# One TensorE-bound attention-and-MLP kernel: the decay row copied by DMA, two tiles mixed transposed, wide unread matmuls, and a new order

## The chip, the cores and the metric

The kernel runs on one core of a Trainium2 chip. A core has a matrix engine (TensorE, PE in the profile, with its weight loads shown apart as PEld), VectorE (DVE), ScalarE (ACT), GpSimd (POOL) and a queue engine (SyncE, SP) that issues most DMAs. TensorE writes to eight banks of PSUM; VectorE and ScalarE read them. Sixteen DMA engines move data between HBM and SBUF.

The metric is the time of one execution in microseconds. The kernel before has a median of 141.36 us in three runs (140.43 to 142.12).

## The reference

Two phases follow each other. The first is a linear attention with a decay per head and channel; the second mixes its output over tokens and channels.

```python
# B, H, S, D = 4, 8, 768, 48
for t in range(S):
    cur = u * k[t] (x) v[t]                    # outer product, D x D per head
    y[t] = r[t] @ (state + cur)
    state = w * state + k[t] (x) v[t]
x = y with the heads side by side              # B, S, 384
theta = x @ w_theta
zr, zi = x * cos(theta), x * sin(theta)
y2 = w_tok_r @ zr + w_tok_i @ zi               # mixes the 768 tokens
un = x + y2
out = un + relu(un @ w_ch)
```

The inputs and the output are float32; r, k and v hold 4.7 MB each, and so does the output.

## The kernel before

The 768 tokens of each of the 4 batches are worked in three groups of 256 tokens, so there are 12 groups, 0 to 11. The scan over time is turned into matmuls. For a group, k and r are multiplied by powers of w (tiles Kw and Rw, L554 and L556, by VectorE or GpSimd), turned by TensorE with an identity ("flip", L493; eight matmuls of 128 columns), copied out of PSUM to KT and RT (L503 on ScalarE, L504 on VectorE), and multiplied with each other ("scores", L605); a mask is applied on the way out (mAT, L614). "outer" (L671) makes the state's update, "diag" (L638) the bonus of u, and "states", "outputs" and "bonus" (L747 to L812) the group's rows of x. x is turned (xT), multiplied with w_theta (L835), and ScalarE takes sine and cosine (L842, L846); VectorE makes z (L850).

When a batch's three z are there, its six tiles of 128 tokens are mixed: 12 matmuls per tile (L872), stationary a 128 x 128 block of the token weights, moving 384 columns of z. VectorE adds x (un, L890), un is turned (uT; by a DMA transpose for groups 0 to 10, by TensorE for group 11), multiplied with w_ch ("chan", L905, three matmuls), and the result is put through relu, added to un and stored.

**The start.** The powers of w need w's logarithm on all 128 partitions. VectorE zeroes a tile (L300), one DMA on SP's queue brings the 1.5 KB of w into its first row (L302), and TensorE multiplies it with a tile of ones ("spread", L311, float32), which puts the row on every partition of a PSUM bank. ScalarE takes the logarithm (L389) and then the powers (L399).

**Unread matmuls.** `unread(k, n, wide)` (L291) issues n matmuls of a tile of zeros into a bank that nothing reads. They keep TensorE at work while it has nothing else to do. At the start there are two blocks ("warm"): 6 and 8 matmuls of 512 columns. The table IDLE puts more behind given tasks: 89 matmuls of 128 columns in all.

**The order.** Nothing is scheduled at run time. A planner, which is not part of the kernel, has written out four tables: ORDER (746 tasks, in the sequence in which they are issued to their engines), WAYS (which of a task's possible engines does it), BANKS (which PSUM bank each product takes) and AFTER (further waits, so that issue order and buffers agree). `Plan.issue` walks through ORDER. Each engine runs its own tasks strictly in that sequence: a task that waits holds up all that stands behind it on its engine. SP runs the loads, the DMA transposes and the stores in the same way. The numbers in `P.add(pe(ns, ...))` are the planner's costs; they do not act on the chip.

The loads go into a ring of 16 buffers (tile ld). In the order before, SP issues k of group 0, the row of w, r of group 0, w and u again for small tables, then r and k of group 1, v of group 0, k and r of group 2 and v of group 1.

**The end.** For group 11 the tiles are not turned by DMA but by TensorE: un on VectorE, flip (three matmuls), copy, chan, and one instruction on VectorE that does relu and the last sum (L920), then the store. On VectorE the last tasks stand in this sequence: un of one tile, a last sum of group 11, the copy of the turned tile, and three more last sums.

Of the kernel before, what the change touches and what calls it, by code (L numbers as in the profile page):

```python
# [30 lines left out]
WARM, WARM_NS = (6, 8), (1280, 1700)  # L31
# [5 lines left out]
ORDER = [  # L37
# [39 lines left out]
]  # L77
# [23 lines left out]


IDLE = [
    (5, 1, 21), (6, 2, 6), (7, 4, 3), (73, 5, 12), (75, 6, 5), (116, 7, 5), (78, 4, 11),
    (88, 6, 4), (124, 1, 3), (96, 7, 9), (107, 6, 7), (51, 6, 3),
]

# [868 lines left out]
```

## Time and profile before

| | |
|---|---|
| median of three runs | 141.36 us (140.43 to 142.12) |
| the profiled execution | 140.2 us |
| its span, first to last instruction | 138.4 us |
| matmuls, and as many weight loads | 1948 |
| busy: TensorE, VectorE, ScalarE, GpSimd | 129.0, 106.6, 81.6, 70.1 us |
| unread matmuls among TensorE's | 103, of which 14 are 512 columns wide |
| moved by DMA | 25.47 MB, 184 GB/s in the mean |

The span lies 1.8 us under the time of the same execution. A profile's busy time of TensorE counts matmuls that overlap each other once, and the length of a single matmul is modelled (326 ns for one that follows the next at 162 ns), so the pace is read from the distance of starts or from a long chain of equal matmuls. "issue" in a view is time in which an engine waited for nothing that the profile shows.

### The profile page before, as it was taken

How to read it: one execution, taken by the hardware profiler on the slowest of the kernel's cores; microseconds unless marked ns; L12 is line 12 of the kernel's file. 1: busy time of each engine (PE TensorE's matmuls, PEld its weight loads, DVE VectorE, ACT ScalarE, POOL GpSimd, SP SyncE). 2: the span in 40 equal slices, each digit the busy share in tenths (PEclk: the TensorE clock that was granted, in tenths of full speed). 3: DMA queues.
4: the chain of work that ended last, by engine and by line, in shares of the span. 5: the costliest groups of instructions: out<-in, count | busy, mean ns of one | idle time of the engine just before them, and what ended most of it. 6: DMA issues, size and time to landing. Idle time of an engine off the chain costs nothing.

```text
span 138.4 us, 4633 instructions
## 1 busy us (share of the span) xinstructions
PE 129.0 (93%) x1948; PEld 87.6 (63%) x1948; DVE 106.6 (77%) x197; ACT 81.6 (59%) x158; POOL 70.1 (51%) x79
## 2 busy tenths in 40 slices
PE   5999996999999969999999999999999999999970
PEld 2848775866776746776666667665657666566630
DVE  6247996889999676989698989799499999353180
ACT  3088878799858459747992174964540738910300
POOL 6003986090075875816546878670519973630310
PEclk9999999999999999999999999999999999999996
DMA  3999599999999971599999999999999792415244
GB/s 97 248 260 259 91 185 205 250 255 243 242 277 210 269 156 20 78 150 192 233 270 237 178 179 147 245 209 188 238 191 265 131 137 85 152 47 147 57 171 171
DMA packets 67199, 25.47 MB, mean 184 GB/s; under 512 B 61801, under 2 KB 67178, under 8 KB 67178
## 3 DMA queue, kind: packets, MB, share of 16 engines
q1 hardware_dynamic: 64746, 22.23, 73.8%
q0 software_dynamic: 2432, 2.95, 13.0%
q8 instruction: 15, 0.25, 0.7%
q14 instruction: 6, 0.05, 0.1%
HBM read 20.06 MB, written 4.72 MB: 179 GB/s over the span
## 4 chain that ended last, share of the span: by engine, by line
PE 75%; DVE 9%; ACT 4%; DMA 3%; issue 3%; POOL 1%; SPq 1%; DVEq 0%; POOLq 0%
PE bank L872 29%; PE bank L493 10%; PE bank L835 8%; PE bank L905 7%; PE bank L291 4%; PE bank L605 4%; DMA ld<-in_r_dram 3%; PE bank L671 3%; PE bank L760 2%; DVE Rw L554 2%; PE bank L812 2%; PE bank L776 2%; PE bank L638 2%; DVE mAT L614 1%; POOL Rw L554 1%
## 5 line engine op out<-in xcount | busy, mean ns | idle before, releaser
L872 PE MATMUL bank<-z,WrT 128*128 128x384 bf16 x144 | 46.9, 326 | 0.1
L872 PE MATMUL bank<-z,WiT 128*128 128x384 bf16 x144 | 46.8, 326 | 0.0
L915 POOL TENSOR_TENSOR fin_all<-fin_all,uu_all 128x384 f32<-128x384 f32 x20 | 17.9, 914 | 24.2 <-ACT fin_all L912 11.4
L554 POOL TENSOR_TENSOR Rw<-ld,rpow 128x768 bf16<-128x768 f32 x6 | 10.9, 1816 | 18.3 <-DVE mask L354 10.1
L614 DVE TENSOR_TENSOR mAT<-bank,mask 128x512 bf16<-128x512 f32 x28 | 18.3, 682 | 2.1 <-PE bank L605 2.0
L890 DVE TENSOR_TENSOR uu_all<-bank,x 128x384 bf16<-128x384 f32 x24 | 13.1, 554 | 8.9 <-PE bank L872 7.1
L872 PEld LDWEIGHTS <-WrT 128*128 128x128 bf16 x144 | 14.0, 98 | 8.1 <-DVE z L850 0.3
L872 PEld LDWEIGHTS <-WiT 128*128 128x128 bf16 x144 | 14.1, 98 | 7.7
L912 ACT ACTIVATE fin_all<-bank 128x384 f32<-128x384 f32 x20 | 9.5, 495 | 12.3 <-issue 8.1
L835 PE MATMUL bank<-Wth,xT 128*128 128x384 bf16 x72 | 14.8, 326 | 1.2 <-issue 1.2
L842 ACT ACTIVATE trig<-bank,pi 128x384 f16<-128x384 f32 x24 | 13.8, 592 | 1.0 <-PE bank L835 0.7
L905 PE MATMUL bank<-Wch,uu_all 128*128 128x384 bf16 x72 | 14.3, 326 | 0.0
L846 ACT ACTIVATE trig<-bank 128x384 f16<-128x384 f32 x24 | 11.9, 499 | 3.9 <-PE bank L835 2.6
L291 PE MATMUL bank<-zero 128*128 128x128 bf16 (+1 forms) x103 | 12.3, 275 | 1.7 <-DVE zero L298 1.7
L850 DVE TENSOR_TENSOR z<-x,trig 128x1536 bf16<-128x1536 bf16 x12 | 11.5, 962 | 2.7 <-ACT trig L846 2.6
L503 ACT ACTIVATE RT<-bank 128x1024 bf16<-128x1024 bf16 x12 | 12.4, 1030 | 2.1 <-PE bank L493 2.0
L614 DVE TENSOR_TENSOR mAT<-bank,mask_c 128x512 bf16<-128x512 f32 x20 | 13.0, 682 | 0.3 <-PE bank L605 0.3
L291 PEld LDWEIGHTS <-zero 128*128 128x128 bf16 x103 | 8.0, 111 | 5.0 <-issue 1.9
L503 ACT ACTIVATE KT<-bank 128x1024 bf16<-128x1024 bf16 x9 | 9.2, 1021 | 2.8 <-PE bank L493 2.8
L647 POOL TENSOR_TENSOR yd<-dg,vb 128x768 bf16<-128x768 f32 x7 | 10.3, 1475 | 0.8 <-DVE Rw L554 0.6
L554 DVE TENSOR_TENSOR Rw<-ld,rpow 128x768 bf16<-128x768 f32 x6 | 7.6, 1261 | 2.2 <-DMA ld<-in_r_dram 2.2
L905 PEld LDWEIGHTS <-uu_all 128*128 128x128 bf16 x72 | 6.5, 97 | 4.1 <-DVE uu_all L504 0.3
(114 smaller groups left out, 226.4 us busy)
## 6 DMA issues: line engine op xcount, KB each, us to landing
ld<-in_r_dram SPq DMA_DIRECT2D x12, 384.0 KB, 5.0
out_dram<-fin_all SPq DMA_DIRECT2D x11, 384.0 KB, 3.1
ld<-in_k_dram SPq DMA_DIRECT2D x7, 384.0 KB, 6.0
ld<-in_v_dram SPq DMA_DIRECT2D x7, 384.0 KB, 8.2
ld<-in_k_dram SPq DMA_DIRECT2D x10, 192.0 KB, 4.1
ld<-in_v_dram SPq DMA_DIRECT2D x10, 192.0 KB, 5.1
fin_all<-in_moe_w_tok_i_dram POOLq DMA_DIRECT2D x1, 384.0 KB, 5.0
x<-in_moe_w_tok_i_dram POOLq DMA_DIRECT2D x1, 384.0 KB, 7.6
```

What stands on the lines that cost most here:

```text
L291: ins = [nc.tensor.matmul(bank_t[k][:, :wide * C].rearrange("p (a c) -> p a c", a=wide), zero, bc(zero, 1, wide), start=True, stop=True, s ...
L493: ins = [nc.tensor.matmul(bank16(tok)[:, i * C:(i + 1) * C], s, ident, is_transpose=True, start=(i == 0), stop=(i == n - 1)) for i, s in e ...
L503: P.add([act(n * C, lambda: nc.scalar.activation(dst, src(), Act.Copy)), dve(n * C, lambda: nc.vector.tensor_copy(dst, src()), 1.0 if pair ...
L554: return eng.tensor_mul(to.rearrange("p j h d -> p h j d")[:, :, :, :D], tokens(i), pw)
L614: mask01[:, j] if pairs else mask_c): nc.vector.tensor_mul(
L835: ins = [nc.tensor.matmul(bank(th)[:, :HD], xT[:, t, dk, :], Wth[:, dk, :], start=(dk == 0), stop=(dk == ND - 1)) for dk in range(ND)]
L842: P.add(act(HD, lambda th=th, t=t, trig=trig: nc.scalar.activation(trig[:, t, 0], bank(th)[:, :HD], Act.Sin, bias=pi2), 144), use=[th], rd ...
L846: P.add(act(HD, lambda th=th, t=t, trig=trig: nc.scalar.activation(trig[:, t, 1], bank(th)[:, :HD], Act.Sin)), use=[th], rd=["sin"], wr=[( ...
L872: ins.append(nc.tensor.matmul(bank(tm)[:, :HD], (WrT, WiT)[ri][:, so, to * C:(to + 1) * C], z[:, so, ri], start=(part == 0 and i == 0), st ...
L890: P.add(dve(HD, lambda tm=tm, t=t, to=to, un=un: nc.vector.tensor_add(un[:, t], bank(tm)[:, :HD], x[:, to])), use=[tm], rd=[("x", xi, pr, ...
L905: ins = [nc.tensor.matmul(bank(tf)[:, :HD], uT[:, t, dk, :], Wch[:, dk, :], start=(dk == 0), stop=(dk == ND - 1)) for dk in range(ND)]
L915: P.add(pool(900, lambda t=t, un=un, fin=fin: nc.gpsimd.tensor_add(fin[:, t], fin[:, t], un[:, t])), rd=[("un", j, t)], wr=[("fin", j, t)] ...
```

## The change

1. **w by one DMA.** The row of w is read 128 times, by one DMA on ScalarE's queue, straight into 128 partitions of SBUF. The zeroing, the tile of ones and the matmul "spread" are gone, and the logarithm reads SBUF in place of PSUM.
2. **The last two tiles in transposed form.** For the two tiles of group 11, each mixing matmul of 384 columns becomes three of 128: stationary a block of z, moving the 128 columns of token weights. The product is un already turned. VectorE adds the turned x (xT) to give uT, which chan reads at once; TensorE turns uT back to un beside it, ScalarE copies that out, and the last sum reads it.
3. **Wide unread matmuls.** The block at the start is one of 10 matmuls of 512 columns. IDLE has 27 of 512 columns and 26 of 128 in place of 89 of 128.
4. **A new order.** ORDER (742 tasks), WAYS, BANKS and AFTER are new throughout. SP issues r of group 0, then k of groups 0 and 1, w and u for the small tables, v of group 0, r of group 1, k and r of group 2, v of group 1. VectorE zeroes the tile that the unread matmuls read as its second instruction. Group 0's r is worked before its k. At the end VectorE's sequence is the sum with xT, then four last sums.

```diff
-WARM, WARM_NS = (6, 8), (1280, 1700)
+(WARM,), WARM_NS = (10,), 2080
...
 IDLE = [
-    (5, 1, 21), (6, 2, 6), (7, 4, 3), (73, 5, 12), (75, 6, 5), (116, 7, 5), (78, 4, 11),
-    (88, 6, 4), (124, 1, 3), (96, 7, 9), (107, 6, 7), (51, 6, 3),
+    (3, 1, 6, 4), (3, 1, 2, 1), (71, 2, 8, 4), (71, 2, 1, 1), (26, 4, 3, 4), (26, 4, 2, 1),
+    (84, 0, 1, 4), (84, 0, 3, 1), (77, 6, 2, 4), (77, 6, 2, 1), (93, 5, 1, 4), (93, 5, 3, 1),
+    (155, 3, 1, 4), (155, 3, 3, 1), (117, 7, 1, 4), (117, 7, 3, 1), (98, 5, 1, 4), (98, 5, 1, 1),
+    (54, 5, 1, 4), (54, 5, 2, 1), (42, 0, 2, 4), (42, 0, 1, 1), (176, 1, 3, 1),
 ]
...
-            for k, n in idle.get(seq, ()):
-                unread(k, n)
+            for a, k, n, wide in idle:
+                if a == seq:
+                    unread(k, n, wide)
...
-        P.add((DVE, 250, False, lambda: nc.vector.memset(w_row, 0.0)), wr=["w_row"],
-              prio=-2.9e4, name="w zero")
-        P.add(sp(lambda: nc.sync.dma_start(out=w_row[:1], in_=rows_of(w, 1)), 400), wr=["w_row"],
-              prio=-1e4, desc=(0, 1, 65), name="w_row", kind="small")
-        P.add((DVE, 160, False, lambda: nc.vector.memset(ones, 1.0)), wr=["ones"], prio=-2.8e4,
-              name="ones")
+        P.add((ACT, 420, False, lambda: nc.scalar.dma_start(out=w_row, in_=rows_of(w, C))),
+              wr=["w_row"], prio=-1.2e4, desc=(2, 8, 70), name="w_row", kind="small")
...
-        P.add(pe(640, lambda: nc.tensor.matmul(
-            bank("w")[:, :HD], ones, w_row.rearrange("p h d -> p (h d)"), start=True, stop=True)),
-            rd=["w_row", "ones"], wr=["spread"], acq=["w"],
-            prio=-1e4, mode=4, name="spread")
...
-        P.add(act(HD, lambda: nc.scalar.activation(
-            lw_f, bank("w")[:, :HD].rearrange("p (h d) -> p h d", h=H), Act.Ln)), use=["w"],
-            rd=["set"], wr=["lw_f"], prio=-200, name="ln")
+        P.add(act_sb(HD, lambda: nc.scalar.activation(lw_f, w_row, Act.Ln)),
+              rd=["set", "w_row"], wr=["lw_f"], prio=-200, name="ln")
...
+                        def mix_t(tm=tm, to=to, part=part):
+                            ins = []
+                            for i in range(4):
+                                so, ri = 2 * part + i // 2, i % 2
+                                for dk in range(ND):
+                                    ins.append(nc.tensor.matmul(
+                                        bank(tm)[:, dk * C:(dk + 1) * C],
+                                        z[:, so, ri, dk * C:(dk + 1) * C],
+                                        (WrT, WiT)[ri][:, so, to * C:(to + 1) * C],
+                                        start=(part == 0 and i == 0 and dk == 0),
+                                        stop=(part == NP - 1 and i == 3),
+                                        skip_group_check=True))
+                            return ins[0], ins[-1]
...
+                    P.add(dve(HD, lambda tm=tm, t=t, uT=uT, xT=xT: nc.vector.tensor_add(
+                        uT[:, t], bank(tm)[:, :HD].rearrange("p (d c) -> p d c", d=ND),
+                        xT[:, t])), use=[tm], rd=[("xT", g % 2)], wr=[("uT", j, t)],
+                        prio=pb + 2 * t, name="un")
+                    flip(un[:, t].rearrange("p (d c) -> p d c", d=ND),
+                         [uT[:, t, dk, :] for dk in range(ND)], ("TU", g, t), pb + 4,
+                         [("uT", j, t)], [("un", j, t)])
+                    continue
...
-                if single:
-                    flip(uT[:, t], [un[:, t, dk * C:(dk + 1) * C] for dk in range(ND)],
-                         ("TU", g, t), pb + 4, [("un", j, t)], [("uT", j, t)])
-
...
-    P.issue(tc, ORDER, WAYS, BANKS, AFTER, dict((a, [(k, n)]) for a, k, n in IDLE), unread)
+    P.issue(tc, ORDER, WAYS, BANKS, AFTER, IDLE, unread)
```

More of the change, by code (lines that the diff above doesn't have):

```diff
@@ L89 @@
-BANKS = ("012345670134520642157630276145326437640516470627105426157321657635642561720436520514325073"
-    "514156714307142530617426137042137251376062501205713265726314652734105632761450146410416237"
-    "56367450261342507510735240735421736502413")
-AFTER = [
[6 rows of a table removed]
[39 rows of a table added]
+]
+WAYS = ("000000000000000000000000000000000000000010010100001001000000000001000000110000000000001100"
+    "100000000000000000000000002000000000000020002000010000000000000000000100000010000000000010"
+    "000000000000001002000000000000000020000000000000000000010100200000000000000010000000101000"
+    "000000011010000000000000000000010000000000000000000000000000000000000000000000000000000000"
+    "001100000000000100101010010000000000000000000000000000000000010000010000000000000000000000"
+    "000000000000000000000000000000000000000000000000000000000000000000000000000000000010000200"
+    "000010000010010000000000000000000000001000000000000100000000000000000000010000000000001001"
+    "000000001000000000000000000000000000000000000000000000000000000000000000000000000000000000"
+    "0000000000000000000000")
@@ L100 @@
+BANKS = ("012345670126304536175235014573654260451730452610526702467032034205420167251075320653712053"
+    "751463201753460210217301273625643515203150476513427605267014265730562540273145417141246315"
+    "026123540712034172564073125604721306452")
+AFTER = [
[6 rows of a table added]
 ]
 IDLE = [
-    (5, 1, 21), (6, 2, 6), (7, 4, 3), (73, 5, 12), (75, 6, 5), (116, 7, 5), (78, 4, 11),
-    (88, 6, 4), (124, 1, 3), (96, 7, 9), (107, 6, 7), (51, 6, 3),
[4 rows of a table added]
 ]
@@ L220 @@
     zero = sb.tile([C, C], BF16, name="zero")
-    ones = sb.tile([C, C], F32, name="ones")
     col_i = sb.tile([C, C], mybir.dt.int32, name="col_i")
@@ L308, in setup @@
         if WARM:
-            P.add(pe(WARM_NS[0], lambda: unread(P.bank_of["warm0"], WARM[0], 4)), rd=["zero"],
+            P.add(pe(WARM_NS, lambda: unread(P.bank_of["warm0"], WARM, 4)), rd=["zero"],
                   acq=["warm0"], prio=-2.1e4, name="warm")
-        P.add(pe(640, lambda: nc.tensor.matmul(
-            bank("w")[:, :HD], ones, w_row.rearrange("p h d -> p (h d)"), start=True, stop=True)),
-            rd=["w_row", "ones"], wr=["spread"], acq=["w"],
-            prio=-1e4, mode=4, name="spread")
-        if WARM:
-            P.add(pe(WARM_NS[1], lambda: unread(P.bank_of["warm1"], WARM[1], 4)),
-                  rd=["zero", "spread"], acq=["warm1"], prio=-1.1e3, name="warm")
         P.add((ACT, 1290, False, lambda: nc.scalar.preload_act_table_set(
@@ L863, in mixing @@
             pb = base + 10 * pr
+            single = g == B * NP - 1
             for t in range(2):
@@ L866, in mixing @@
                 tm = ("mx", b, to)
+                if single:
+                    xT = xTs[g % 2]
+                    for part in range(NP):
+                        def mix_t(tm=tm, to=to, part=part):
[11 more added lines that the diff above has]
+                            return ins[0], ins[-1]
+                        P.add(pe(678, mix_t), rd=[("z", zj, part), ("Wr", to), ("Wi", to)],
+                              acq=[tm] if part == 0 else [], use=[] if part == 0 else [tm],
+                              wr=[] if part == 0 else [tm], prio=pb + 2 * t, spare=3,
+                              name="mix")
+                    P.add(dve(HD, lambda tm=tm, t=t, uT=uT, xT=xT: nc.vector.tensor_add(
[6 more added lines that the diff above has]
+                    continue
                 for part in range(NP):
@@ L892, in mixing @@
                         rd=[("x", xi, pr, t)], wr=[("un", j, t)], prio=pb + 2 * t, name="un")
-            single = g == B * NP - 1
             if not single:
```

9 lines of the change are left out of this document (removed), and 90 rows, old and new, of tables (AFTER, ORDER).

## The prediction

> **What bounds the kernel now.** I read the page's busy row first, then the busy time by stages, then the waits of TensorE, and then the chain that ended last.
>
> ```profile
> span 138.4 us, 4633 instructions
> PE 129.0 (93%) x1948; PEld 87.6 (63%) x1948; DVE 106.6 (77%) x197; ACT 81.6 (59%) x158; POOL 70.1 (51%) x79
> ...
> q8 instruction: 15, 0.25, 0.7%
> ```
>
> ```profile
> 17.73:23.33 5.60, 4.51 (x132) 3.41 (x129) 5.28 (x10) 4.68 (x9) 4.26 (x4) 1.00 1.16 195
> 44.84:51.20 6.36, 5.17 (x141) 3.75 (x133) 5.01 (x10) 3.16 (x7) 4.83 (x4) 1.00 1.06 234
> 59.13:63.33 4.20, 4.20 (x137) 2.88 (x137) 3.60 (x6) 2.55 (x6) 0.34 (x1) 1.00 0.93 145
> 63.34:131.65 68.31, 68.26 (x831) 44.67 (x820) 53.01 (x86) 36.16 (x78) 39.04 (x38) 1.00 0.87 176
> ```
>
> (Columns: stage, its length, busy time and instructions of PE, PEld, DVE, ACT, POOL, granted clock, share of the DMA engines, GB/s.) In the last stage TensorE is busy 68.26 of 68.31 us, so there nothing but the length of its own program sets the time. What can be gained lies ahead of it, in the waits inside the first two stages shown, and behind 131.65.
>
> ```profile
> PE bank L291 <- DVE zero L298: 1.7, 1, 1.7
> PE bank L835 <- issue: 1.2, 1, 1.2
> PE bank L671 <- issue: 1.0, 1, 1.0
> ```
>
> The two waits called "issue" are for nothing that another engine does. To see what they are I cut the stage table at them and count instructions.
>
> ```profile
> 0.00:23.32 23.32, 20.00 (x350) 14.63 (x350) 16.37 (x48) 15.28 (x26) 11.23 (x21) 1.00 0.92 192
> 23.33:51.03 27.70, 26.18 (x511) 18.73 (x512) 24.58 (x42) 21.08 (x38) 13.10 (x15) 1.00 1.11 243
> ```
>
> From one wait to the next TensorE starts 511 matmuls and 512 weight loads, 1023 instructions, nearly four times 256; and 3896 instructions over the 15 packets of the instruction queue are 260 each. So the program comes in pieces of about 256 instructions (128 matmuls), and both waits stand at the first instruction of a piece. Counted back from there, the piece before the first wait was entered at 17.73 and the one before the second at 44.84: from entering a piece to having the next took 5.60 and 6.36 us, with the DMA engines full (1.16 and 1.06). The piece from 59.13 to 63.33 lasted 4.20 us and nothing waited, with 0.93. A piece that TensorE gets through in under some 5.6 to 6.4 us while the DMA engines are full runs dry.
>
> **The change part by part.**
>
> *The start.* The chain in order of time, to the first unread matmuls and on:
>
> ```profile
> 1.02 0.38 DVE z L300
> 1.39 0.14 DVE ones L304
> ...
> 1.67 4.98 PE bank L291 x27
> 6.65 0.75 PE bank L311 x2
> 7.42 0.50 ACT z L389
> 7.94 1.13 ACT kpow L399 x2
> ...
> 17.72 0.50 PE bank L291 x9
> ```
>
> The 27 unread matmuls are 6 of 512 columns and 21 of 128, 45 blocks of 128: 4.98 / 45 = 111 ns a block, against 0.50 / 9 = 56 ns later. Only behind them came "spread", the logarithm, two powers, and
>
> ```profile
> 10.20 0.61 PE L493 MATMUL bank<-ident,Kw 128*128 128x128 bf16 x8 [0.33 <-DVE Kw L554]
> ```
>
> the first real flip at 10.20. Afterwards TensorE starts with (10 + 6) x 4 + 2 = 66 blocks: 45 at 111 ns and 21 at 56 ns are 6.2 us, from about 1.1 (VectorE writes the zeros before other things now, and the 0.38 and 0.14 us ahead of them go), until 7.3. Beside that, w's copy goes out at about 0.75 on ScalarE's queue. No DMA of the trace has its form; the nearest are stores of the same 128 rows of 1.5 KB, and loads of its size in short rows:
>
> ```profile
> out_dram<-fin_all SPq DMA_DIRECT2D x2, 192.0 KB, 1.9
> ```
>
> ```profile
> ld<-in_k_dram SPq DMA_DIRECT2D x10, 192.0 KB, 4.1
> ```
>
> I take 3.0 us and keep 1.9 and 4.1: w lands at 2.7 to 4.9. Then 0.50 for the logarithm, 1.13 for two powers and about 0.95 for Rw end at 5.3 to 7.5, under the unread matmuls. So the first flip stands at about 7.6, 2.6 us earlier. If that cover is gone each microsecond of lateness counts in full.
>
> Against it stands what comes behind the first flip: 59 unread blocks before (3.3 us at 56 ns), now 21 x 4 + 24 = 108 (6.05 us): +2.75. The two cancel. What is left is that scores, masks and copies of group 0 are ready some 2 us earlier against the same place in TensorE's program, which shortens its waits there. By the chain, each kind of work has a pace where it runs undisturbed:
>
> ```profile
> 44.44 0.30 PE bank L747 x4
> 44.74 0.50 PE bank L760 x32
> 45.25 0.33 PE bank L776 x4
> 45.58 0.57 PE bank L605 x32
> 46.15 0.27 PE bank L671 x30
> ...
> 47.18 0.34 PE bank L493 x6
> ...
> 48.50 0.18 PE bank L638 x8
> ```
>
> At such paces the program from the first flip to matmul 478 (29.35 us) is 12.4 us of work and 3.3 of unread blocks; 19.15 us passed, 1.0 of it the wait for the piece. The other 2.5 us are small waits and restarts. I take 1.0 of them as gone; the bounds are 2.5 gained and 1.0 lost, the latter if the loads of group 1 (r is fifth on SP's queue now, third among the loads before) hold the flips.
>
> *The pieces.* Wide unread matmuls take a quarter of the instructions for the same time, and the new order spreads the rest. I counted the new order in pieces of 128 matmuls, at the paces above. Matmuls 223 to 350 come to 35 scores (0.62), 18 outputs (0.28), 32 outer (0.29), 8 diag (0.18), 8 states (0.60), 4 bonus (0.33), 18 flips (1.02), 2 wide and 3 narrow unread (0.61), 3.9 us; before, the same numbers held 3.65. With the 0.9 us of other waits that stood there (5.60 - 1.02 - 3.65) it is 4.8 against 5.6: 0.8 us dry. The later pieces with full DMA engines come to 6.2, 6.3, 6.2, 5.8 and 5.8 (the shortest of before was 5.2), and with some 0.3 us of small waits each they are within 0.3 us of 6.4: together 0.2. So 2.2 us of waits become 1.0: -1.2. Bounds: none left if pieces come as quickly as at 59.13 (-2.2), 3.1 if all take 6.4 and no small wait helps (+0.9). The Trainium skill (Runtime: NRT & Kernel Launch, Instruction fetch mechanics) says that instructions come in blocks of 256 and that crossing into the next is mostly hidden. The trace agrees with the block and not with the hiding; by that sentence this term would be nothing.
>
> *The narrow mixing.* 24 matmuls of 384 columns become 72 of 128.
>
> ```profile
> 69.29 0.94 PE bank L493 x16
> ...
> 119.45 9.75 PE bank L872 x60
> ```
>
> 16 flips of 128 columns, each with its own weights, took 59 ns apiece; a mixing matmul took 162.5. 72 x 59 less 24 x 162.5 is +0.35 us, on the path; with flips at 56 ns (8 in 0.45) it would be +0.15. I take +0.2, and 0.2 more for the flip of w and u, which now falls behind the first real flip. The Trainium skill (TensorE: Matmul & The Clock Gate, Back-to-back issue gap) gives about 81 ns for a stream of 128-column matmuls with weight loads; by it the term is +1.9.
>
> *The end.*
>
> ```profile
> 131.75 0.57 DVE uu_all L890
> ...
> 133.86 1.04 DVE fin_all L920 x2
> ```
>
> ```profile
> 133.24 1.67 DVE L920 SCALAR_TENSOR_TENSOR fin_all<-bank,uu_all 128x384 f32<-128x384 f32 x3
> ```
>
> From the last mixing matmul (131.65) to the last sum (134.91) VectorE did un, one sum, a copy and three sums, 3.26 us. Afterwards it does the sum with xT and four sums: 0.1 + 0.57 + 4 x 0.56 = 2.9, and if the third sum waits for chan behind two other chans and for ScalarE's copy, 3.0. So -0.25; the bounds are -0.4 and +0.5. The last store and the landing behind it stay.
>
> *SP's queue and the rest.* One 1.5 KB load leaves SP (0.32 us of issue), w's copy adds 192 KB, some 0.75 us at 250 GB/s, to DMA engines with a share of 0.92 up to 23.32; it is in the range of the waits in front. The 0.52 us that VectorE no longer spends on the zeroing and the ones lie where it waits for the powers anyway, and count for the unread matmuls' start alone.
>
> **Sum**, against the profiled execution (140.2 us, span 138.4): first flip -2.6, unread blocks +2.75, narrow mixing and the flip of w and u +0.4, waits in front -1.0, pieces -1.2, end -0.25: -1.9. That is 138.3 for such an execution and 139.5 from the median, which lies 1.2 above it. Pieces that come late are the likeliest reason that the three runs differ by 1.7 us, and these get rarer, so I go a little under the latter: **139.2 us**.
>
> **The rivals.**
>
> *More than that.* TensorE keeps its lead: front waits -2.5 and both piece waits gone (-2.2) in place of -1.0 and -1.2 give 137.0 from the median. For it speaks that VectorE and ScalarE could do nothing of group 0 until the powers came at 9.07; against it that the loads of group 1 land no earlier. 0.14.
>
> *Pieces are no shorter where it counts.* Matmuls 223 to 350 still price at 3.9 us, and the waits stay at 2.2, or the front gains nothing: 140.2 to 142.0, within 1%. The page's rule that crossings are hidden ends here too, since then the two waits had another cause and stay. 0.23.
>
> *The narrow mixing costs 81 ns each*, as the skill's figure has it: 1.7 more than summed, 140.9. The flips at 59 ns speak against it. 0.04.
>
> *A load comes late on SP's queue* (the other side).
>
> ```profile
> 93.66 0.71 SPq L510
> 94.47 0.52 SPq L932
> 95.04 4.77 DMA ld<-in_r_dram
> 99.83 0.97 DVE Rw L554
> 100.85 0.62 PE bank L493 x8
> ```
>
> The r of group 9 stands on SP behind a transpose and a store, is issued at 95.04, lands 4.77 later, and TensorE meets its flip at 100.85 with almost no wait. In the new order other stores and transposes stand ahead of each load. A load behind a transpose that waits 2 us for VectorE comes 2 us later, and TensorE, whose tasks keep their sequence, stands still for that. It decides from the point where such a load lands over 1.9 us later than TensorE's place for it; two such give +4 and 143.5. 0.13.
>
> *w's copy is slow.* 128 reads of the same 1.5 KB could be far slower than the rows above. Over 5 us of landing the first flip moves with it, and at 9 us (four more) more than all is lost: 143.2. 0.08. That the change doesn't do what it says (the copy, the wide matmuls) can't be: they are in the program.
>
> **How the numbers follow.** About 1% (1.4 us) is what a measurement of this kernel can tell. The forecast, 138.3 to 139.9, has 0.38; with the 0.14 it is faster by over 1% (under 139.95) at 0.52. 0.23 + 0.04 are within 1%: 0.27. 0.13 + 0.08 are slower: 0.21. The range reaches over the better case (137.0, and 0.6 for its bounds) down to 136.4 and, on the other side, past 142.8 into the smaller half of the late loads: 142.9; outside lie 0.03 and 0.15.
>
> **What would show it.** First real flip at 7 to 8 us, w's copy landed before 5; "issue" waits of TensorE about 1.0 in all, the largest near the 350th matmul; TensorE busy throughout from 51 us; the narrow mixing at 56 to 60 ns; last mixing matmul to last sum 2.9 to 3.0 us. Wrong would be a first flip past 9, issue waits over 2 us, or a wait of TensorE for a DMA behind 50 us.

## The result, and the profile after

The changed kernel takes 139.05 us (median of 20 runs, 138.38 to 140.82) where the kernel before takes 140.55 us beside it (20 runs, 139.46 to 142.12): a ratio of 0.9895, with a 95% interval of 0.9866 to 0.9924. It is faster by about 1.5 us. Run again beside the first experiments, the same program gave 139.18 us and 0.9934 (0.9897 to 0.9971).

Ratios are taken over the executions within 1.5% of their kernel's fastest, so a ratio can differ a little from the quotient of the medians beside it, and the profile shown is for the same reason that of the second time (139.74 us, span 138.0) and not that of the first (140.82 us, its slowest). First its busy times and TensorE's waits (line, what it waited for, us in total, times, longest):

```profile
PE 128.6 (93%) x1954; PEld 86.8 (63%) x1954; DVE 108.2 (78%) x198; ACT 80.5 (58%) x154; POOL 70.7 (51%) x80
```

```profile
PE bank L483 <- DVE Rw L544: 2.0, 1, 2.0
PE bank L293 <- DVE zero L300: 1.0, 1, 1.0
PE bank L737 <- DVE mAT L604: 0.5, 1, 0.5
PE bank L483 <- DVE Kw L544: 0.5, 1, 0.5
PE bank L825 <- DMA xT<-x: 0.3, 1, 0.3
```

Both waits called "issue", 2.2 us in the profile of before, are gone. In their place stands one wait of 2.0 us ahead of the first real flip (L483). The busy time by stages shows the same, first of the kernel before, then of the changed one:

```profile
0.00:10.00 10.00, 8.21 (x47) 4.96 (x47) 4.16 (x26) 3.83 (x7) 2.10 (x12) 1.00 0.85 199
10.00:20.00 10.00, 9.53 (x241) 7.98 (x241) 9.19 (x19) 8.40 (x15) 6.70 (x7) 1.00 0.91 182
20.00:30.00 10.00, 8.70 (x205) 6.60 (x202) 8.14 (x17) 8.24 (x17) 5.23 (x8) 1.00 1.13 229
30.00:51.00 21.00, 19.74 (x375) 13.82 (x374) 19.43 (x32) 15.89 (x28) 10.29 (x10) 1.00 1.10 243
...
70.00:131.00 61.00, 60.95 (x739) 39.70 (x737) 47.74 (x79) 30.13 (x63) 34.35 (x32) 1.00 0.85 172
```

```profile
0.00:10.00 10.00, 6.98 (x30) 3.04 (x31) 4.50 (x26) 3.94 (x6) 2.07 (x12) 1.00 0.64 164
10.00:20.00 10.00, 9.41 (x182) 6.55 (x180) 9.89 (x19) 5.37 (x10) 5.07 (x7) 1.00 1.06 210
20.00:30.00 10.00, 9.26 (x217) 6.77 (x216) 8.18 (x16) 8.62 (x18) 6.53 (x8) 1.00 1.15 225
30.00:51.00 21.00, 20.78 (x378) 15.07 (x377) 19.65 (x31) 13.61 (x26) 12.43 (x11) 1.00 1.12 244
...
70.00:131.00 61.00, 60.36 (x772) 40.76 (x771) 45.64 (x76) 32.26 (x63) 30.08 (x33) 1.00 0.87 172
```

From 20 to 51 us TensorE (the first busy time of a row) stood idle 2.56 us before and 0.96 us now; in the first 20 us it stood idle 2.26 before and 3.61 now, and from 70 to 131 us 0.05 before and 0.64 now. In these two executions the start and the last of these stages gave back what the middle gained. For the start, the chain in order of time (start, length, what) says why:

```profile
0.73 5.21 DMA z<-in_w_dram
5.96 0.53 ACT z L380
6.52 1.13 ACT rpow L389 x2
7.67 0.97 DVE Rw L544
...
8.77 0.62 PE bank L483 x8
```

The chain now begins with w's copy, which takes 5.21 us. The first flip follows at 8.77 (10.20 before).

At the other end, VectorE's rows of the timeline (start, length, what):

```profile
131.74 0.56 DVE L878 TENSOR_TENSOR uu_all<-bank,xT 128x384 bf16<-128x384 f32 x1 [1.92 <-PE bank L866]
132.29 2.18 DVE L934 SCALAR_TENSOR_TENSOR fin_all<-bank,uu_all 128x384 f32<-128x384 f32 x4
```

VectorE's last stretch is 131.74 to 134.47, 2.73 us; before it was 131.75 to 134.91, 3.16 us. So in these two executions TensorE comes to the end at the same time, and the 0.4 us by which the spans differ is the end's. The two executions lie 0.46 us apart (140.2 and 139.74), the medians of the runs 1.0 to 1.5; the one shown is among the longer ones of the changed kernel. How the rest of that difference is shared out can't be read from one execution of each; the experiments below price the parts by medians.

### The profile page after: what moved, and what is told of

It reads as the page before. It is cut to its first block, busy times and chain, and to the rows that moved or that the text cites. A ratio compares the mean times of both kernels' runs of the same rounds, so it can differ in the third digit from the quotient of the medians.

```text
span 139.0 us, 4656 instructions
## 1 busy us (share of the span) xinstructions
PE 129.2 (93%) x1954; PEld 87.1 (63%) x1954; DVE 109.2 (79%) x198; ACT 80.6 (58%) x154; POOL 70.8 (51%) x80
## 4 chain that ended last, share of the span: by engine, by line
PE 55%; DMA 22%; ACT 5%; POOL 5%; SPq 3%; issue 3%; DVE 3%; DVEq 0%; POOLq 0%
PE bank L891 23%; PE bank L483 8%; DMA z<-in_moe_w_tok_i_dram 6%; DMA ld<-in_v_dram 5%; PE bank L919 5%; DMA ld<-in_k_dram 4%; PE bank L825 4%; PE bank L595 4%; DMA z<-in_w_dram 4%; DMA xT<-x 3%; PE bank L866 3%; PE bank L661 2%; ACT KT L493 2%; SPq L432 2%; POOL fin_all L929 1%
## 5 line engine op out<-in xcount | busy, mean ns | idle before, releaser
L891 PE MATMUL bank<-z,WrT 128*128 128x384 bf16 x132 | 43.0, 326 | 0.0
L891 PE MATMUL bank<-z,WiT 128*128 128x384 bf16 x132 | 42.9, 326 | 0.0
L840 DVE TENSOR_TENSOR z<-x,trig 128x1536 bf16<-128x1536 bf16 x12 | 14.1, 1172 | 6.1 <-ACT trig L836 5.0
L891 PEld LDWEIGHTS <-WiT 128*128 128x128 bf16 x132 | 12.9, 98 | 6.8
L909 DVE TENSOR_TENSOR uu_all<-bank,x 128x384 bf16<-128x384 f32 x22 | 11.9, 551 | 4.8 <-PE bank L891 4.7
L293 PE MATMUL bank<-zero 128*128 128x512 bf16 (+1 forms) x63 | 13.9, 361 | 1.0 <-DVE zero L300 1.0
L637 POOL TENSOR_TENSOR yd<-dg,vb 128x768 bf16<-128x768 f32 x9 | 13.3, 1473 | 2.0 <-DVE Kw L544 1.0
L544 POOL TENSOR_TENSOR Rw<-ld,rpow 128x768 bf16<-128x768 f32 x4 | 7.2, 1808 | 6.8 <-DVE z L840 6.3
L293 PEld LDWEIGHTS <-zero 128*128 128x128 bf16 x63 | 5.8, 107 | 7.5 <-issue 3.6
L611 POOL TENSOR_TENSOR PD<-RT,KT 128x1024 bf16<-128x1024 bf16 x4 | 8.5, 2123 | 3.2 <-ACT KT L493 1.8
```

The costliest lines, as they stand in the source:

```text
L293: ins = [nc.tensor.matmul(bank_t[k][:, :wide * C].rearrange("p (a c) -> p a c", a=wide), zero, bc(zero, 1, wide), start=True, stop=True, s ...
L544: return eng.tensor_mul(to.rearrange("p j h d -> p h j d")[:, :, :, :D], tokens(i), pw)
L637: return eng.tensor_mul(yd.rearrange("p a b d -> p (a b) d"), wide(dg, D), vb.rearrange("p a b d -> p (a b) d"))
L840: P.add(dve(4 * HD, lambda trig=trig, pr=pr: nc.vector.tensor_mul(z[:, 2 * pr:2 * pr + 2], bc(x[:, 2 * pr:2 * pr + 2], 2, 2), trig), 2.0, ...
L891: ins.append(nc.tensor.matmul(bank(tm)[:, :HD], (WrT, WiT)[ri][:, so, to * C:(to + 1) * C], z[:, so, ri], start=(part == 0 and i == 0), st ...
L909: P.add(dve(HD, lambda tm=tm, t=t, to=to, un=un: nc.vector.tensor_add(un[:, t], bank(tm)[:, :HD], x[:, to])), use=[tm], rd=[("x", xi, pr, ...
```

## The experiments

Ratios are to the kernel before in the same session, with 95% intervals; the changed kernel itself stands at 0.9895 and 0.9934.

### The changed kernel again

The program is the same, and its numbers stand above.

> The changed kernel itself once more, beside the others on one chip: 138.6 to 139.4 us, 1% under before. Its trace shows whether the waits of TensorE in the first profiled execution (0.5 to 0.7 us each, 4 us in all behind the first flip) are usual: I expect under 3 us in all, and at most 0.5 us of 'issue' waits.

0.9934 (0.9897 to 0.9971) beside 0.9895 (0.9866 to 0.9924) says how far one kernel moves between two sessions: 0.4%. Under 3 us of waits and at most 0.5 us of "issue" waits were expected; the profile has no "issue" wait, and those shown above behind the first flip come to 1.3 us.

### Pieces: wide unread matmuls alone, in the old order

```diff
 # kernel before
-                unread(k, n)
+                if n >= 4:
+                    unread(k, n // 4, 4)
+                if n % 4:
+                    unread(k, n % 4)
```

> The kernel before, with its unread matmuls behind the tasks issued as 512-column ones where four of them go together (17 wide and 21 narrow in place of 89 narrow; the same columns, the same order, nothing left out). Theory of the pieces: the boundaries of TensorE's program move by 50 matmuls against the tasks, so no 'issue' wait is left at the 29th matmul of outer of group 1 or inside theta of group 3; waits, if any, stand at matmuls 222, 350, 734 or 990 (the pieces ending there price at 4.1, 4.1, 5.0 and 4.8 us). With two short pieces under full DMA engines the waits stay about 1 to 2.5 us in all, and the time within 1% of before (139.5 to 141.5). Rival, that something at those two operations is waited for: both waits stay at the same operations with 1.0 and 1.2 us.

139.6 us, ratio 0.9997 (0.9965 to 1.0028): no difference. The longest waits of its profile behind the start:

```profile
PE bank L750 <- POOL Sd L697: 0.6, 1, 0.6
PE bank L496 <- DMA z<-in_moe_w_tok_i_dram: 0.4, 1, 0.4
```

No "issue" wait is left, so those waits belonged to the place of the boundaries and not to the two operations they stood at. But what TensorE no longer loses to pieces it loses to other engines in the old order: up to 131 us it stood idle 5.08 us in the profile of before and 4.65 here, although 2.2 us of waits are gone.

### Pieces: narrow unread matmuls in the new order

```diff
 # changed kernel; likewise for every row of IDLE
-    (3, 1, 6, 4), (3, 1, 2, 1), (71, 2, 8, 4), (71, 2, 1, 1), ...
+    (3, 1, 24, 1), (3, 1, 2, 1), (71, 2, 32, 1), (71, 2, 1, 1), ...
```

> The changed kernel with each wide unread matmul as four of 128 columns, so part 3 is undone with the same columns. By my account of the pieces, the 81 further pairs of matmul and weight load shift every boundary: they stand now at matmuls 222, 350 and 478 of a program whose pieces price at 3.8, 4.2 and 4.7 us, under the 5.6 it took to have the next. Waits called issue come back at one or two of these three matmuls, 1.0 to 2.2 us in all, and the time is 139.6 to 141.0. Rival, after the wide matmuls in the kernel before: waits come back, but stand in the place of other waits, and the time stays within 0.4 us of the changed kernel. Second rival: no issue wait comes back; then the boundaries did not set them.

140.73 us, ratio 1.0025 (0.9990 to 1.0060). The same columns in more instructions cost the whole gain. Its profile is of an execution of 142.35 us, so what counts is the places of its waits and not their sizes. TensorE's waits, and the busy time up to the first and from one to the next:

```profile
PE bank L623 <- issue: 1.5, 1, 1.5
...
PE bank L590 <- issue: 0.9, 1, 0.9
...
PE bank L745 <- issue: 0.4, 1, 0.4
```

```profile
0.00:17.36 17.36, 14.25 (x222) 10.48 (x222) 11.96 (x40) 6.85 (x12) 5.00 (x17) 1.00 0.86 194
...
17.37:23.28 5.91, 4.99 (x128) 3.84 (x128) 5.54 (x10) 5.53 (x11) 4.85 (x7) 1.00 1.13 183
23.29:29.74 6.45, 4.99 (x128) 4.11 (x128) 4.52 (x10) 4.51 (x7) 3.66 (x3) 1.00 1.02 215
```

Three waits came back, behind matmuls 222, 350 and 478 (the first row counts 222 up to the first of them), the three places that were written down. Between them lie exactly 128 matmuls and 128 weight loads, at other operations (L745, L590, L623) than in the kernel before. The two full pieces took 5.91 and 6.45 us with the DMA engines full, in line with the 5.6 and 6.4 read from the profile of before. The Trainium skill (Runtime: NRT & Kernel Launch, Instruction fetch mechanics) calls such crossings mostly hidden; these three were not, and cost 0.4 to 1.5 us each.

The traces also show what TensorE waits for. The instruction queue (q8 in the page) moves packets of 16,384 bytes, one for each boundary. The kernel before has 15 such packets, and this run, with 162 more matmuls and weight loads than the changed kernel, has 16. The profiles of this case hold nine "issue" waits: two before, three here, two with w's copy in the old order, and one each with the copy on SP's queue and with the first "spread". They stand behind matmul 222, 350, 478 or 861, a multiple of 128 apart to within one record, and each ends 1.3 to 1.7 us after such a packet has come in. In the kernel before the packet for 350 starts 3.3 us after the piece ahead of it is entered, with the DMA engines full; the one during the piece from 59.13, where nothing waited, starts after 0.65 us.

### w's copy alone, in the old order

```diff
 # kernel before; the row, its zeroing, the ones and "spread" are gone
+        P.add((ACT, 420, False, lambda: nc.scalar.dma_start(out=w_row, in_=rows_of(w, C))),
+              wr=["w_row"], prio=-1.2e4, desc=(2, 8, 70), name="w_row", kind="small")
```

> The kernel before with part 1 of the change alone: w copied to 128 partitions by one DMA on ScalarE's queue, first in the order; zeroing, ones and the matmul that spread the row are gone; the same unread columns, the same order otherwise. The copy lands near 5.6 us as in the changed kernel's trace, the powers end near 7.4, the first real flip stands near 9 instead of 10.2. Theory (the start is worth what TensorE's program behind it keeps): 0.5 to 1.2 us faster than before, piece waits of 1 to 2 us as before. Rival, that the start is worth nothing because the loads of the first groups come 1.3 us later behind the copy: within 0.3 us of before.

142.13 us, ratio 1.0130 (1.0072 to 1.0187): slower, on the wrong side of the expectation. Of the profile (an execution of 142.86 us) the start, from the timeline:

```profile
7.91 0.20 PE L342 MATMUL bank<-ident_f,wu 8*128 8x8 f32 x1 [1.79 <-DMA wu<-in_u_dram]
8.04 3.29 PE L230 MATMUL bank<-zero 128*128 128x512 bf16 x11
11.12 1.06 PE L423 MATMUL bank<-ident,Kw 128*128 128x128 bf16 x8
```

Beside the copy SP spends 2.77 us on issuing the row of w for the small tables (0.81 in the kernel before) and so issues the row of u at 4.68 in place of 3.08. TensorE waits 1.79 us for it, and then does its second block of unread matmuls ahead of the first real flip, which starts at 11.12 in place of 10.20. That block takes 3.29 us in place of 2.07, for the granted clock is 0.68 from 8 to 10 us and 0.50 from 10 to 12, behind the wait, though no unread matmul was left out. Doing away with "spread" (0.75 us) saved nothing. Two piece waits remain, 1.7 us behind matmul 350 and 0.7 behind 861, where they stood in the kernel before by the count, although with "spread" gone this is two matmuls further on in the work. How much of the 1.3% is the late row, the clock or the pieces isn't separated.

### w's copy first on SP's queue

```diff
 # changed kernel
-        P.add((ACT, 420, False, lambda: nc.scalar.dma_start(out=w_row, in_=rows_of(w, C))),
+        P.add(sp(lambda: nc.sync.dma_start(out=w_row, in_=rows_of(w, C)), 420),
```

> The changed kernel with w's copy on SP's queue ahead of all loads instead of on ScalarE's beside them; nothing else changed. If the copy was slow because it shared the DMA engines with two loads, it lands at 3 to 4 us instead of 5.6, the powers end 1 to 2 us earlier, r of group 0 lands where it did (its 7.06), so the first real flip stands at about 8.0 to 8.2 instead of 8.46, and the time is 0 to 0.5 us under the changed kernel's. If 128 reads of one row are slow by themselves, it lands at 5 us or later all the same, r behind it at 7 or later, and the time is the same or up to 0.5 us longer.

138.64 us, ratio 0.9908 (0.9877 to 0.9938), no difference that the runs can tell from the changed kernel. At the head of the queue the copy still takes 4.2 us (row below), between the 3 to 4 and the 5 us that the two expectations named. The first flip stands at 7.78, about 1 us earlier, and one piece wait of 0.4 us stands behind matmul 350.

### The copy reads 128 different rows

```diff
 # changed kernel
-        P.add((ACT, 420, False, lambda: nc.scalar.dma_start(out=w_row, in_=rows_of(w, C))),
+        P.add((ACT, 420, False, lambda: nc.scalar.dma_start(
+            out=w_row, in_=moe_w_ch[:C].rearrange("p (h d) -> p h d", h=H))),
...
-        P.add(act_sb(HD, lambda: nc.scalar.activation(lw_f, w_row, Act.Ln)),
+        P.add(act_sb(HD, lambda: nc.scalar.activation(
+            lw_f, w_row, Act.Ln, bias=nine, scale=1e-6)),
```

The copy has the same form and size but another source, so the decay is a constant and not the reference's w.

> One look at the price of the copy by itself: the changed kernel, with the copy's 128 reads of one 1.5 KB row replaced by reads of 128 different rows of the same length (the first 128 rows of w_ch), in the same DMA; the logarithm is taken of a constant, so the decay is wrong and the time is read for the DMAs alone. If reading one row 128 times is what makes the copy slow, it lands at 3 to 4 us instead of 5.6 to 5.9 and the first load behind it at 5 to 5.5 instead of 7.1 to 7.4. If its size or the shared engines are, it lands at 5.5 to 6 as before.

136.75 us in a single execution (before: 139.84, a median), span 135.0. The DMA issues of the first 12 us (KB, us from issue to landing), in turn of the changed kernel, of the copy on SP's queue and of this one:

```profile
z<-in_w_dram ACTq DMA_DIRECT2D x1, 192.0 KB, 5.2
```

```profile
z<-in_w_dram SPq DMA_DIRECT2D x1, 192.0 KB, 4.2
```

```profile
z<-in_moe_w_ch_dram ACTq DMA_DIRECT2D x1, 192.0 KB, 2.9
```

A copy of 128 different rows lands in 2.9 us, which is the 3.0 that the prediction took; 128 reads of one row take 4.2 to 5.2. SP's timeline shows a second cost, in the row of the two loads (k of groups 0 and 1) that it issues beside the copy; first of the changed kernel, then of this one:

```profile
1.25 4.67 SPq L432 DMA_DIRECT2D ld<-in_k_dram  x2
```

```profile
1.26 2.31 SPq L435 DMA_DIRECT2D ld<-in_k_dram  x2
```

Beside the slow copy SP needs 4.67 us to issue two loads, until 5.92, just before the copy lands at 5.94; here it needs 2.31, until 3.57, and the copy lands at about 3.6. It is 1.57 where only the 1.5 KB row goes ahead of them (the next experiment). All that stands behind on SP's queue is late by as much: r of group 1 is issued at 8.02 in the changed kernel and at 5.82 here. With the quick copy the first flip stands at 6.63, 2.1 us earlier, and the wait for Rw (2.0) is no longer among TensorE's:

```profile
1.02 5.51 PE bank L294 x18
...
6.63 0.62 PE bank L486 x8
```

### One row and "spread" in the new order

```diff
 # changed kernel: the 1.5 KB row first on SP's queue, spread behind n of the ten wide unread matmuls
+                a = unread(P.bank_of["warm0"], n, 4)[0]
+                nc.tensor.matmul(bank_t[7][:, :HD], ones, w_row[:1].rearrange("p h d -> p (h d)"),
+                                 start=True, stop=True)
+                return a, unread(P.bank_of["warm0"], 10 - n, 4)[1]
```

First with n = 5 and all unread matmuls kept:

> The changed kernel with w's row brought by a 1.5 KB DMA, first on SP's queue, and put on all partitions by TensorE with a one-row tile of ones, between the 5th and the 6th of the ten wide unread matmuls at the start; order and all else as changed. Theory, that the copy holds up the loads by 2 to 3 us: r of group 0 lands near 4.7 instead of 7.1 to 7.4, the powers end near 5.6, so the first real flip stands at the end of the unread matmuls, about 8.0, and the waits of TensorE for Rw and Kw in front go from 1.8 to 2.5 us to under 0.8; 0.4 to 1.5 us under the changed kernel. Rival, that the copy costs nothing that counts: within 0.3 us of the changed kernel.

140.09 us, ratio 1.0028 (0.9994 to 1.0063): the gain is lost, where a time 0.4 to 1.5 us under the changed kernel's was expected. Its chain:

```profile
3.34 1.57 PE bank L311 x2
4.91 5.02 PE bank L294 x13
9.93 0.65 PE bank L491 x8
```

"Spread" takes 1.57 us here (0.75 in the kernel before, where it came after 5 us of matmuls and multiplied all 128 rows in place of one), and the 13 unread matmuls behind it take 5.02. These are 46 blocks of 128 columns at 109 ns, the pace of the first 5 us of the kernel before (111). The starts of single matmuls show the step from 0.43 to 0.21 us a wide one at 10.2 us here and at 5.1 in the changed kernel. No load stands in the chain any more; the unread matmuls themselves now hold the first flip. Why the quicker pace comes so late behind "spread" wasn't tested by itself.

Then with n = 4, and one wide unread matmul behind the ten in place of six wide and two narrow ones:

> As the one before, with the spreading after the 4th wide unread matmul and only one wide one behind the ten instead of six wide and two narrow. If the unread matmuls at the start hold up real work there, the first flip comes at 6.5 to 7 us and the time falls by a further 0.5 to 1.3 us; if the program behind is bound by the loads or by VectorE, TensorE waits for the same time later and nothing is gained (within 0.3 us).

137.95 us, ratio 0.9875 (0.9835 to 0.9915), an interval that overlaps those of the changed kernel. Its chain:

```profile
2.91 1.57 PE bank L306 x2
4.48 3.10 PE bank L289 x7
7.58 0.87 PE bank L486 x8
```

The chain's first flip is at 7.58, 1.2 us ahead of the changed kernel's. Five wide and two narrow unread matmuls fewer in front of the first flip, 22 blocks or 2.4 us at 109 ns, are the main difference to the run before: the flip is 2.35 us earlier and the median 2.14 us lower.

### No unread matmuls behind the first flip

```diff
 # changed kernel
-IDLE = [(3, 1, 6, 4), (3, 1, 2, 1), (71, 2, 8, 4), ... ]
+IDLE = [(3, 1, 6, 4), (3, 1, 2, 1)]
```

> The changed kernel without the unread matmuls behind the first real flip (48 instructions, 108 blocks of 128 columns, 6 us by the pace of 56 ns); those at the start stay. By my account of TensorE's program the 6 us would be paid in full unless TensorE would have waited there: if they only fill waits, the time is within 0.5 us of the changed kernel; if they hold up real work, it falls by 1 to 3 us; if they keep TensorE's pace at 56 ns a block, it rises, and the trace shows flips at 110 ns in the front.

139.62 us, ratio 0.9980 (0.9947 to 1.0014): not faster than with them but 0.5 to 0.9% slower, though its interval overlaps that of the changed kernel's second measurement. What is left out is 45 instructions (21 wide, 24 narrow), not the 48 of the expectation; the 108 blocks are right. Its waits, and the stage from 10 to 20 us:

```profile
PE bank L478 <- DVE Kw L539: 2.3, 1, 2.3
PE bank L478 <- DVE Rw L539: 1.9, 1, 1.9
PE bank L590 <- ACT KT L488: 1.9, 2, 1.0
```

```profile
10.00:20.00 10.00, 7.27 (x150) 6.33 (x151) 9.89 (x19) 4.91 (x9) 4.78 (x7) 0.66 1.06 204
```

The waits for Kw, Rw and KT grow by 3.6 us in all (the first two from 2.5 to 4.2, KT from none to 1.9), and the granted clock of that stage is 0.66 where it is 1.00 in the stages of the other kernels shown above. Of the 6.05 us of unread blocks left out, then, 3.6 come back as waits; the flips of Rw and Kw between 15 and 18 us take 0.92 to 1.06 us at the lower clock, where those of the changed kernel take 0.61 or 0.62. How much slower the run would be by either alone isn't separated.

### The last two tiles as before, in the new order

```diff
 # changed kernel
-                                for dk in range(ND):
-                                    ins.append(nc.tensor.matmul(
-                                        bank(tm)[:, dk * C:(dk + 1) * C],
-                                        z[:, so, ri, dk * C:(dk + 1) * C],
-                                        (WrT, WiT)[ri][:, so, to * C:(to + 1) * C],
+                                ins.append(nc.tensor.matmul(
+                                    bank(tm)[:, :HD], (WrT, WiT)[ri][:, so, to * C:(to + 1) * C],
+                                    z[:, so, ri], start=(part == 0 and i == 0),
...
+                    flip(uT[:, t], [un[:, t, dk * C:(dk + 1) * C] for dk in range(ND)],
+                         ("TU", g, t), pb + 4, [("un", j, t)], [("uT", j, t)])
```

> The changed kernel with part 2 undone: the last two tiles are mixed by 24 matmuls of 384 columns, VectorE adds x, TensorE turns un, ScalarE copies it out, then chan. By the two traces the narrow mixing costs 0.06 us and the end gained 0.43 (3.26 to 2.83 from last mixing matmul to last sum), so this is 0.2 to 0.4 us slower than the changed kernel, with 3.0 to 3.3 us from last mixing matmul to last sum. Rival: the end is short because VectorE has four sums in a row and no copy; ScalarE still does the copy here, so the end stays at 2.8 to 2.9 and the time within 0.1 us.

140.02 us, ratio 0.9975 (0.9939 to 1.0011), slower than the changed kernel by 0.4 to 0.8% (0.6 to 1.1 us; 0.2 to 0.4 was expected), though its interval overlaps that of the second measurement. VectorE's end, from the timeline:

```profile
131.79 0.56 DVE L834 TENSOR_TENSOR uu_all<-bank,x 128x384 bf16<-128x384 f32 x1 [1.89 <-PE bank L825]
132.39 1.05 DVE L888 SCALAR_TENSOR_TENSOR fin_all<-bank,uu_all 128x384 f32<-128x384 f32 x2
134.29 1.05 DVE L888 SCALAR_TENSOR_TENSOR fin_all<-bank,uu_all 128x384 f32<-128x384 f32 x2 [0.85 <-PE bank L873]
```

3.55 us in place of 2.73: VectorE stands 0.85 us before the last two sums, because chan has to wait for the turned tile. The rival fell: four sums in a row do not make the end short by themselves, the transposed form does. 0.82 us is more than the 0.43 against the kernel before. In this order TensorE does six chan matmuls (131.69 to 132.68) ahead of the last flip, which stood at 132.37 in the kernel before; ScalarE's copy follows at 133.04, after it stood idle for 1.41 us.

### A better start

```diff
 # one row and spread (n = 4), ORDER and IDLE
-... 68, 19, 10, 71, 150, 2, 72, 67, 151, 110, 69, ...
+... 68, 19, 67, 71, 150, 2, 72, 151, 110, 10, 69, ...
-(71, 2, 8, 4), (71, 2, 1, 1),
+(71, 2, 2, 4), (71, 2, 1, 1),
```

> The changed kernel with the 1.5 KB row, the spread behind four wide unread matmuls and one wide one behind the ten, and further: VectorE makes group 0's Kw right behind its Rw, ahead of the mask and of the copy of RT, and two wide unread matmuls stand behind the first flip in place of eight. Kw is done near 8.1 in place of 10.5, KT is copied out near 10.5 in place of 12.4. Theory: VectorE's sequence behind the powers sets the front; scores start 1.5 us earlier and the time is 136.5 to 137.3. Rival: the loads of group 1 (k lands 7.8, r 10.9) and VectorE's later work set it; the earlier start turns into waits for Kw, Rw and mAT up to 30 us, and the time stays at 137.6 to 138.4.

137.81 us, ratio 0.9836 (0.9808 to 0.9865): the fastest of all that computes the reference, 2.4 us under the kernel before beside it. The time is what the rival gave; 0.9836 can't be told from 0.9875 with these intervals. One of its waits, and its chain:

```profile
PE bank L624 <- DVE vb L536: 1.0, 1, 1.0
```

```profile
8.33 1.23 DVE RT L457
...
11.21 0.47 DVE vb L536
...
12.15 0.70 DVE PD L574
```

The start now runs through VectorE from 8.33 to 12.85 with hardly a gap, and TensorE waits 1.0 us for vb. Moving Kw ahead helped little because VectorE's later work is late then, which is one half of the rival. Of its other half, the loads of group 1, the chain shows nothing, and of the waits that it named up to 30 us only mAT's stands there (0.5 us).

## Why the prediction was right, and where it was not

The time came out at 139.05 for 139.2 forecast. Some of that closeness is luck: the kernel before has a median of 140.55 in 20 runs and not the 141.36 that the forecast started from, so the gain is 1.5 us for 2.2 forecast. More of it is luck in the sum: its two largest terms, -2.6 for the first flip and +2.75 for unread blocks, were both off and cancelled each other. The direction, "faster by over 1%", holds by the first measurement (1.05%) and not by the second (0.66%). By the steps:

1. **"The pieces", -1.2.** The mechanism was right: the waits end with the instruction packets and keep to the count. They went altogether in the trace, -2.2, one of the bounds; with the copy on SP's queue, in the same order, 0.4 us stands behind matmul 350, near where the largest was forecast. I had summed matmuls 223 to 350 to 4.8 us with their small waits and expected 0.8 us dry. The stage that holds 128 weight loads up to that place, in the changed kernel:

```profile
20.36:25.93 5.57, 4.93 (x139) 3.53 (x128) 5.27 (x10) 5.31 (x10) 4.66 (x6) 1.00 1.19 204
```

   It lasted 5.57 us, as long as a piece took to come before (5.60): TensorE was slowed by other things there, the wait for mAT (0.5) among them, and so the piece was just in time: its packet had come in 1.4 us before, about the least that passes elsewhere before such a wait ends. A part of the 2.2 us was not won but spent elsewhere. The narrow unread matmuls put back into the new order cost 0.9 to 1.3% (1.0025 against 0.9934 and 0.9895); it is the largest of the parts that I priced.
2. **"The start", first flip -2.6.** Here the step failed: 10.20 became 8.77, so -1.4. The term that was mis-sized is w's copy: 3.0 us taken, 1.9 and 4.1 kept, 5.2 measured. The rival "w's copy is slow" named the reason and set the point from which it decides at 5 us of landing; it landed at 5.94, and the first flip moved with it, as that rival said. The rows it was bounded by move different rows of memory, and so does the run that lands in 2.9. What neither the term nor the rival has is the queue behind the copy: r of group 1 was issued at 8.02 us (3.76 in the kernel before, 5.82 beside the quick copy), where the forecast gave the copy 0.75 us of the DMA engines' time.
3. **"Unread blocks", +2.75.** Wrong as a cost. Without the 45 instructions behind the first flip the kernel is no faster, rather slower: 3.6 of their 6.05 us come back as waits, and the granted clock falls to 0.66 for 10 us. Only unread matmuls ahead of the first flip can hold it, and they did where the loads were early (9.93 in the first kernel with "spread").
4. **"Waits in front", -1.0.** Not found in this trace: the idle time of TensorE in the first 51 us went from 4.82 to 4.57, although 2.2 us of piece waits left it. The start took 2.0 of it back at the first flip.
5. **"The narrow mixing", +0.2.** Of the changed kernel's chain:

```profile
127.22 2.01 PE bank L866 x36
```

   36 matmuls of 128 columns in 2.01 us are 55.8 ns each, so 72 less 24 of 162.5 ns are +0.12, near the +0.15 that stood beside the +0.35 in the working. The 81 ns of the Trainium skill (TensorE: Matmul & The Clock Gate, Back-to-back issue gap) and the rival made of it do not hold here.
6. **"The end", -0.25.** -0.43, at the better bound (-0.4). Undoing the transposed form alone costs 0.82 us at the end.
7. **"A load comes late on SP's queue".** Not at the size that rival needed. TensorE waits 0.3 us for xT, a DMA, at 116 us, which I had named as a mark of being wrong; from 70 to 131 us it is idle 0.64 us where it was 0.05. That is small against the 1.9 us from which the rival decides, but it is lost, and the sum had nothing for it.

Left open is how the gain of the medians is made up beyond the pieces and the end: the parts undone one by one cost 0.9 to 1.3% (wide unread matmuls) and 0.4 to 0.8% (transposed tiles), which together is already the whole gain or more, and w's copy by itself is no gain in either order. What the order alone brings was not run.

## What to carry to other kernels

Count instructions as well as time: where TensorE's waits stand a fixed number of matmuls apart, the test is to move the boundary and see whether the wait stays with the count. Fewer and longer instructions removed such waits here, but in the old order that alone gained nothing: other waits took their place. A copy of one row to all partitions should be priced by a run of its own, since stores and loads of the same size said little of it, and what stands behind it on the queues belongs to the price. Unread matmuls cost nothing here behind the first real work and cost in full ahead of it, so the quicker start paid only when those ahead of it were made fewer.

## What the runs showed of the hardware

- 128 reads of the same 1.5 KB row took 4.9 to 5.2 us to land on ScalarE's queue beside loads and 4.2 at the head of SP's; 128 reads of different rows took 2.9 on ScalarE's. Why the same row is slower was not tested. Two loads that SP issued beside the copy took 4.67 us to issue, 2.31 beside the quick one.
- Every "issue" wait of TensorE stands a multiple of 128 matmuls and 128 weight loads from the next and ends 1.3 to 1.7 us after a packet of 16,384 bytes on the instruction queue. Where the DMA engines were full, 5.6 to 6.45 us passed from one such boundary to the end of the wait at the next.
- The granted clock fell to 0.66 from 10 to 20 us where TensorE had waits of 1.9 and 2.3 us and one of 0.9 in a row and no unread matmuls between. It also fell with all unread matmuls in place, to 0.50 from 10 to 12 us, in the profile with w's copy in the old order, behind one wait of 1.79 us.
- "Spread" (two float32 instructions) took 0.75 us after 5 us of matmuls, with 128 rows, and 1.57 us after 1.9 or 2.3 us of them, with one row. Behind the latter, unread matmuls went on at 109 to 111 ns a block up to the first flip, at 7.58 and 9.93 us; in the changed kernel the pace doubled at 5.1 us.
